# An attention and feed-forward kernel whose program order is planned in advance: new first loads, one weight for all feature products, an added dependency in the plan, new priorities

## The chip, the cores and the metric

The kernel runs on one core of a Trainium2 chip. The metric is the device time of one execution in microseconds (us), as the median of several executions. Beside each changed kernel the kernel before was run on the same chip. PE is the matmul engine, PEld its weight loads, DVE the vector engine, ACT the scalar engine, POOL the general one, and SP issues most transfers.

## The reference, cut to what matters

```python
def _attn_ref(q, k, v, w_phi):               # 8 batches, 8 heads, 576 rows, head_dim 64
    def phi(x):
        proj = einsum('bhsd,df->bhsf', x, w_phi)            # 128 features
        proj = proj - max(abs(proj), axis=-1, keepdims=True)
        return concatenate([exp(proj), exp(-proj)], axis=-1)
    q_p, k_p = phi(q), phi(k)
    kv  = einsum('bhsf,bhsd->bhfd', k_p, v);   z = sum(k_p, axis=2)
    num = einsum('bhsf,bhfd->bhsd', q_p, kv)
    den = einsum('bhsf,bhf->bhs', q_p, z) + 1e-6
    return num / den

def _moe_ref(x, g_ln, w_ch1, w_ch2):         # x: 8 x 576 x 512, all heads side by side
    xn = (x - mean(x)) / sqrt(var(x) + 1e-6) * g_ln
    return x + maximum(xn @ w_ch1, 0) @ w_ch2               # 512 -> 2048 -> 512
```

Inputs and output are fp32; the kernel multiplies in bf16.

## The kernel before

The work is cut into 32 *units* of two heads, eight to each pair of batches. When a pair's eight units are done, its layer norm and its feed-forward block can start. So the units of the second, third and fourth pair run beside the feed-forward products of the pair before. In each unit, k and q are transposed (units 0 to 7 on PE, the later ones by a transposing DMA), multiplied by w_phi into PSUM, and read there. For k, three instructions read the same PSUM tile of 128 x 1024 values: DVE takes the row maxima of the absolute values, and ACT takes exp(+) and exp(-). The exps leave the maximum out; it is put in later as a factor on v, so the first exp does not need it as data.

The order of all this is not written by hand. A small list scheduler in Python (class `Order`) plays the whole kernel through with planned durations, and at each moment gives a free engine the ready operation of the lowest rank. The rank is the latest start that the plan allows plus an offset from a table. When it is done, the operations are emitted in the planned order, and each engine runs its own list in that order on the chip:

```python
class Order:
    def add(self, engine, us, rank, emit, r=(), w=(), acquire=None, release=None, lag=0.2, due=None):
        ...                          # dependencies: on the last writer of every key read or written
    def run(self):
        ...
        for op in done:              # in the order in which the plan started them
            op.emit()
```

These are the operations of a k tile. `us` is the planned duration, `r` and `w` what is read and written. As declared, `exps(0)` and the maxima both only read `ps_key`, so in the plan they may run at the same time:

```python
        add("PE", mm(4, 256), rk(nm, n), products, r=[("qkT", n % QB, i), ("T", n % QB)],
            w=[ps_key] + [("EB", t, n % 2) for t in range(2) if i], acquire=("A", 1))
        add("DVE", 1.14, rk(nm + ".max", n), maxima, r=[ps_key], w=[("m", i, n % 3)],
            release=None if i else ("A", 1))
        ...
        add("ACT", 0.92, rk("k.exp", n), lambda: exps(0), r=[ps_key],
            w=[("EB", 0, n % 2)])
        add("ACT", 0.92, rk("k.exp", n), lambda: exps(1),
            r=[ps_key, ("m", i, n % 3), ("EB", 0, n % 2)],
            w=[("EB", 1, n % 2)], release=("A", 1))
```

And this is the start: w_phi on the POOL queue, three weights made of it, and the first k transpose behind the "mixed" transpose, which needs the tails of q and k (the last 64 rows of each head):

```python
    nc.gpsimd.dma_start(out=wphi_f[0:D, :], in_=w_phi)
    nc.gpsimd.dma_start(out=wphi_f[D : 2 * D, :], in_=w_phi)
    ...
    for nm, s0, s1 in (("wbk", 1.0, 1.0), ("wbx", 2.0, 1.0), ("wbq", 2.0, 2.0)):
        wb[nm] = t_ = consts.tile([P, 2, F], BF16, name=nm)
        ...
        add("PE", mm(1, 128), rank, mixed, r=data, w=[("qxT_ps", n), ("T", j), "T"], acquire=("B", 1))
        ...
        for which in ((1,), (0,)) if n == 0 else ((1, 0),):      # k first, then q
```

## Time and profile before

| | before |
|---|---|
| median time | 409.37 us (408.7 to 410.06, three executions) |
| profiled span | 407.0 us |
| PE busy | 368.2 us, 90 % |
| first k product | 7.99 us |
| first feed-forward product of pair 1, of pair 2 | 49.5 us, 162.4 us |

The page of the profile of the kernel before opens with the span and the busy time of each engine. Then each digit is the busy share, in tenths, of one of 40 equal slices of the span (here 10.2 us each).

```profile
span 407.0 us, 8895 instructions
PE 368.2 (90%) x3315; PEld 232.3 (57%) x3366; DVE 250.2 (61%) x548; ACT 268.7 (66%) x595; POOL 195.5 (48%) x343
...
PE   3998878599999988799999999998999999999994
...
DVE  4688988497989989776666889747373820000000
ACT  3878978379687777674958777867574644444421
```

A 9 is not necessarily full: it means 90 % or more. The view by windows of the kernel before resolves that. Columns: stretch in us, its length, busy us and count of PE, PEld, DVE, ACT and POOL, granted PE clock, mean busy share of the DMA engines, GB/s.

```profile
0.00:50.00 50.00, 41.40 (x670) 37.30 (x677) 36.85 (x86) 37.23 (x82) 33.46 (x78) 1.00 1.00 250
50.00:80.00 30.00, 20.42 (x209) 13.65 (x210) 21.06 (x48) 21.26 (x48) 18.36 (x40) 0.94 1.16 219
80.00:170.00 90.00, 82.65 (x753) 51.11 (x762) 80.54 (x180) 67.61 (x153) 53.94 (x89) 1.00 0.67 170
170.00:230.00 60.00, 56.53 (x512) 35.81 (x522) 42.52 (x83) 42.80 (x95) 32.49 (x52) 1.00 0.52 128
230.00:290.00 60.00, 57.66 (x488) 34.98 (x494) 43.22 (x93) 46.03 (x107) 31.46 (x52) 1.00 0.38 92
```

PE is short of work up to 80 us.

The start on PE, from the timeline of the kernel before (start, duration, engine, line, operation, tiles; in brackets the idle time before and what ended it):

```profile
6.25 0.27 PE L477 MATMUL qxT_ps<-ident,qx_114 128*128 128x128 bf16 x1 [4.43 <-DMA qx_114<-in_k_dram]
...
6.87 0.40 PE L567 MATMUL px<-wbx,qkT_136 128*128 128x256 bf16 x1
...
7.99 1.06 PE L610 MATMUL pm<-wbk,qkT_136 128*128 128x256 bf16 x4
```

PE's two longest waits, from the list of waits of the kernel before (total us, times, longest):

```profile
PE pm L610 <- DMA qkT_136<-b_1_140: 4.9, 1, 4.9
PE qxT_ps L477 <- DMA qx_114<-in_k_dram: 4.4, 1, 4.4
```

The first is the stall near 75 us: one DMA transpose that takes very long. In the chain of waits of the kernel before it is this piece (start, duration):

```profile
59.15 17.20 DMA qkT_136<-b_1_140
```

### The profile page before, as it was taken

What the parts mean: (1) busy time and instruction counts of PE and PEld (TensorE: products, weight loads), DVE (VectorE), ACT (ScalarE), POOL (GpSimd) and SP (SyncE); (2) the same over time, 40 slices, a digit from 0 to 9 for tenths busy, and PEclk for the clock granted to TensorE, in tenths of its full rate; (3) what the DMA queues carried; (4) which work ended last, traced back from release to release, by engine and by line L of the source; (5) the groups of instructions that cost most, each with busy time, mean ns of one, the idle gap of its engine ahead of it and who ended that gap; (6) DMA issues with size and microseconds to landing.
All of it is one profiled execution on the core that took longest, in us unless ns stands there. A gap on an engine that the chain in (4) does not pass through costs nothing.

```text
span 407.0 us, 8895 instructions
## 1 busy us (share of the span) xinstructions
PE 368.2 (90%) x3315; PEld 232.3 (57%) x3366; DVE 250.2 (61%) x548; ACT 268.7 (66%) x595; POOL 195.5 (48%) x343
## 2 busy tenths in 40 slices
PE   3998878599999988799999999998999999999994
PEld 2988845356565645465565655665656555555541
DVE  4688988497989989776666889747373820000000
ACT  3878978379687777674958777867574644444421
POOL 4658768364776726444563744664535211111032
PEclk9999999899999999999999999999999999999998
DMA  7999999957486485966362328421000340101012
GB/s 197 281 228 278 256 229 225 203 157 191 100 226 212 104 219 125 218 104 198 71 195 57 101 78 182 127 52 30 27 28 27 76 119 31 47 27 52 27 52 78
DMA packets 92347, 53.28 MB, mean 131 GB/s; under 512 B 58992, under 2 KB 87664, under 8 KB 92304
## 3 DMA queue, kind: packets, MB, share of 16 engines
q1 hardware_dynamic: 86672, 48.05, 46.6%
q0 software_dynamic: 4288, 4.26, 6.2%
q8 instruction: 26, 0.43, 0.4%
q10 hardware_dynamic: 1344, 0.40, 0.4%
q14 instruction: 17, 0.14, 0.1%
HBM read 36.77 MB, written 9.44 MB: 114 GB/s over the span
## 4 chain that ended last, share of the span: by engine, by line
PE 44%; issue 15%; DVE 15%; DMA 12%; ACT 8%; POOL 3%; SPq 1%; POOLq 0%; ACTq 0%; DVEq 0%
PE hT_ps L989 17%; PE ch_ps L1020 13%; PE pm L610 4%; DMA qkT_136<-b_1_140 4%; ACT eb_141 L627 4%; DMA qkT_138<-b_0_139 3%; ACT eb_142 L627 3%; DVE numc L787 2%; PE n_bank L717 2%; DVE m_144 L617 2%; DVE m_143 L617 2%; POOL o L1039 2%; DVE numc L793 2%; DVE m_145 L617 2%; DMA qk_110<-in_q_dram 1%
## 5 line engine op out<-in xcount | busy, mean ns | idle before, releaser
L1020 PE MATMUL ch_ps<-w_129,hT 128*128 128x512 bf16 x537 | 145.4, 379 | 1.8 <-DVE xT_134 L890 0.2
L989 PEld LDWEIGHTS <-w_128 128*128 128x128 bf16 x768 | 73.2, 98 | 60.6 <-issue 4.5
L999 ACT ACTIVATE hT<-hT_ps 128x384 bf16<-128x384 f32 x127 | 62.5, 492 | 58.6 <-PE hT_ps L989 58.4
L803 POOL TENSOR_TENSOR x<-numc,rden 128x384 bf16<-128x384 f32 (+3 forms) x88 | 45.8, 539 | 76.8 <-DVE rden L797 76.4
L1020 PEld LDWEIGHTS <-hT 128*128 128x128 bf16 x576 | 53.8, 98 | 43.6 <-issue 0.3
L1039 POOL TENSOR_TENSOR o<-o,x 128x512 f32<-128x512 f32 x23 | 26.7, 1159 | 78.0 <-ACT o L1033 72.4
L989 PE MATMUL hT_ps<-xT_135,w_128 128*128 128x384 bf16 x256 | 52.0, 326 | 0.7 <-ACT hT L999 0.7
L989 PE MATMUL hT_ps<-xT_133,w_128 128*128 128x384 bf16 x256 | 50.1, 329 | 2.1 <-ACT hT L999 1.7
L989 PE MATMUL hT_ps<-xT_134,w_128 128*128 128x384 bf16 x256 | 51.2, 326 | 0.5 <-DVE o L1028 0.3
L997 DVE TENSOR_SCALAR hT<-hT_ps 128x384 bf16<-128x384 f32 x65 | 35.8, 553 | 13.5 <-PE hT_ps L989 12.5
L627 ACT ACTIVATE eb_141<-pm 128x1024 bf16<-128x1024 f32 x32 | 32.7, 1029 | 12.4 <-DVE m_144 L617 4.8
L627 ACT ACTIVATE eb_142<-pm 128x1024 bf16<-128x1024 f32 x32 | 32.8, 1026 | 11.5 <-DVE m_143 L617 3.5
L688 ACT ACTIVATE ea_126<-pt 128x1024 bf16<-128x1024 f32 x32 | 32.2, 1047 | 4.4 <-PE pt L682 2.4
L688 ACT ACTIVATE ea_124<-pt 128x1024 bf16<-128x1024 f32 x32 | 32.0, 1039 | 3.4 <-PE pt L682 3.1
L617 DVE TENSOR_REDUCE m_144<-pm 128x8 f32<-128x1024 f32 x22 | 26.8, 1219 | 11.9 <-ACT eb_142 L627 4.7
L617 DVE TENSOR_REDUCE m_143<-pm 128x8 f32<-128x1024 f32 x22 | 26.7, 1217 | 9.8 <-ACT eb_141 L627 6.8
L617 DVE TENSOR_REDUCE m_145<-pm 128x8 f32<-128x1024 f32 x20 | 24.3, 1218 | 10.4 <-PE pm L610 4.2
L1028 DVE SCALAR_TENSOR_TENSOR o<-ch_ps,rstd_165,x 128x512 f32<-128x512 f32 x2 | 1.5, 750 | 41.4 <-PE ch_ps L1020 41.4
L787 DVE TENSOR_TENSOR numc<-num,em 128x390 f32<-128x390 f32 (+1 forms) x40 | 20.6, 514 | 5.8 <-PE num L763 5.6
L1192 PE MATMUL n_bank<-wz 128*128 128x120 bf16 x313 | 22.4, 218 | 1.1 <-DVE KV L725 1.0
L641 POOL TENSOR_TENSOR vv<-v_109,em 128x512 bf16<-128x512 f32 x12 | 12.6, 1049 | 17.9 <-issue 9.2
L793 DVE TENSOR_TENSOR numc<-numc,num 128x390 f32<-128x390 f32 (+1 forms) x40 | 20.5, 515 | 0.3
(221 smaller groups left out, 656.0 us busy)
## 6 DMA issues: line engine op xcount, KB each, us to landing
out_dram<-o SPq DMA_DIRECT2D x32, 256.0 KB, 2.3
qk_108<-in_k_dram SPq DMA_DIRECT2D x12, 256.0 KB, 3.2
v_109<-in_v_dram SPq DMA_DIRECT2D x12, 256.0 KB, 3.8
qk_108<-in_q_dram SPq DMA_DIRECT2D x11, 256.0 KB, 4.8
qk_110<-in_k_dram SPq DMA_DIRECT2D x10, 256.0 KB, 4.5
qk_110<-in_q_dram SPq DMA_DIRECT2D x10, 256.0 KB, 5.7
v_111<-in_v_dram SPq DMA_DIRECT2D x10, 256.0 KB, 4.7
qk_112<-in_k_dram SPq DMA_DIRECT2D x10, 256.0 KB, 4.8
```

Source lines behind the costliest of these rows:

```text
L617: nc.vector.reduce_max(out=u["m"][:, i, 0:MX], in_=u["pm", i], axis=AX.X, apply_absolute_value=True)
L627: nc.scalar.activation(u["EB"][:, t, 0:MX, :], u["pm", 1], AF.Exp, scale=(1.0, -1.0)[t])
L688: nc.scalar.activation(u["EA"][:, t, 0:1024], u["pt"], AF.Exp, scale=(1.0, -1.0)[t])
L787: nc.vector.tensor_tensor(out=view(st["numc"]), in0=view(st["ps"][1]), in1=bcast(e, 3 if shape else 2, D1), op=ALU.mult,)
L793: nc.vector.tensor_add(out=st["numc"], in0=st["numc"], in1=st["ps"][0])
L803: nc.gpsimd.tensor_tensor(out=dst, in0=st["numc"][ps_, i : i + n, 0:D], in1=bcast(st["rden"][ps_, i : i + n], 2, D), op=ALU.mult,)
L989: nc.tensor.matmul(st["ps"], w1_sb[:, kc, jj * P : (jj + 1) * P], xT_bufs[(pair * NR + r) % XB][:, kc::KC, :], start=(kc == 0), stop=(kc = ...
L997: nc.vector.tensor_relu(h_sb, st["ps"])
L999: nc.scalar.activation(h_sb, st["ps"], AF.Relu)
L1020: nc.tensor.matmul(ch[t], hT[r, jj][:, rt * P : (rt + 1) * P], w2_sb[:, jj, :], start=(jj == 0), stop=(jj == JC - 1),)
L1039: nc.gpsimd.tensor_tensor(out=ch["o", t], in0=ch["o", t], in1=x[:, t, :], op=ALU.add)
L1192: nc.tensor.matmul(warm, wz, wz[:, 0:WN], start=False, stop=False, skip_group_check=True)
```

## The change

Its intent is to start the first exps earlier, and to have a better order of work after that. It has four parts. (a) The start: w_phi moves to the ACT queue, and one block-diagonal weight serves all products (q's factor of two goes into a small exp). k transposes no longer wait for tails, the load order is set, and one of two table loads goes away. (b) In the plan, the first exp of k also waits for the maxima. (c) The plan has a new model of how long a transfer holds its queue. (d) All priorities are new.

```diff
-DUE, BLOCK = 34.0, 26.0
+DUE = 24.7
+BLOCK = 127.5
 OFF = (
-        "load": -75.5, "trans": -3.0, "trans.copy": -34.0, "mixed": -14.9, ...
+        "load": 291.2, "trans": 434.7, "trans.copy": 59.4, "mixed": -235.7, ...
   ... (all three tables, every number)
-            us = [2.0 if callable(us) else us for us in op.us]
+            us = [0.6 if callable(us) else us for us in op.us]
-    nc.gpsimd.dma_start(out=wphi_f[0:D, :], in_=w_phi)
-    nc.gpsimd.dma_start(out=wphi_f[D : 2 * D, :], in_=w_phi)
+    nc.scalar.dma_start(out=wphi_f[0:D, :], in_=w_phi)
+    nc.scalar.dma_start(out=wphi_f[D : 2 * D, :], in_=w_phi)
-    wb = {}
-    for nm, s0, s1 in (("wbk", 1.0, 1.0), ("wbx", 2.0, 1.0), ("wbq", 2.0, 2.0)):
-    ...
+    wbk = consts.tile([P, 2, F], BF16, name="wbk")
+    nc.vector.memset(wbk, 0.0)
+    for i in range(2):
+        rows = slice(i * D, (i + 1) * D)
+        nc.vector.tensor_copy(out=wbk[rows, i, :], in_=wphi_f[rows, :])
-        def held(now, free):
-            return max(us, free.get(kind, 0.0) - now)
-        add(queue, held if tiles else us, rank, emit, r=r, w=(key, *w))
+        def issued(now, free):
+            both = free.get(other, 0.0) > now or backlog[other] > 0
+            wait = max(0.0, free.get(kind, 0.0) - now) + backlog[kind] * (0.046 + 0.094 * both)
+            backlog[kind] += packets
+            return max(us, wait) if tiles else us
+        add(queue, issued, rank, emit, r=r, w=(key, *w))
+        if n:
+            add_mixed()
+            add_main((1, 0))
+        else:
+            add_main((1,))         # k block of the first unit
+            add_mixed()
+            add_main((0,))
-                    wbk if i else wbq, start=True, stop=True,
+                    wbk, start=True, stop=True,
-        add("ACT", 0.92, rk("k.exp", n), lambda: exps(0), r=[ps_key],
+        add("ACT", 0.92, rk("k.exp", n), lambda: exps(0), r=[ps_key, ("m", i, n % 3)],
             w=[("EB", 0, n % 2)])
   ... (first loads reordered; one explicit table load)
```

## The prediction

> **What bounds it now.** The page of the profile gives a span of 407.0 us with PE (matmul) busy 368.2 us (90%), ACT 268.7, DVE 250.2. The 10 us windows split it into three stages. (a) 0 to 80 us: PE is often filler or idle; the warm-up matmuls on `wz` (313 of them) fill gaps until 45 us. (b) 80 to about 165 us: PE is mostly busy, but it runs out of feed-forward work at 150 to 170 us (8.21 and 7.72 us busy of 10), because the second pair's attention is not ready; DVE is busy 10.00 of 10 us in 150 to 160. (c) From 170 us PE is nearly full, and from 320 us it is 9.95 of 10. So the end is set by how early the second pair reaches its first feed-forward product (162.4 us in the timeline). That is paced by DVE and ACT, plus stalls.
>
> The stalls that count: the first transpose starts only at 6.25 us (list of waits: PE waits 4.4 us for the `qx` tail load), although the k block, 3.0 to 3.7 us from issue, should be there by about 4.2 us. The first exps of k stand at 10.35 and 13.06 us. At 71.5 to 76.4 us PE waits 4.9 us for the DMA transpose `qkT_136`; in the chain of waits that DMA is 17.2 us long. Its issue alone took 8.1 us, behind 1 MB of loads and beside the w2 load; DMA share is 1.2 to 1.4 there. DVE and ACT idle too (3.9 and 4.0 us busy of 10).
>
> **What the change does.** w_phi goes from the POOL queue to the ACT queue; k transposes no longer wait for tails; six weight scalings on DVE (0.21 to 0.62 us) become two; one table load (1.28 us) goes away. k transposes can start near 4.2 us and k products near 5.3 us instead of 7.99. q now queues behind two w_phi issues (about 0.5 us each) and the mixed tile lands about 1 us later, but that is not first in line now. The Trainium skill (DMA: Bandwidth & Descriptors, "Issuing engines are not separate DMA queues") says that more queues save issue time, not bandwidth; the trace agrees as far as DMA share is already over 1 from 10 us on, so I count only latency. Estimate: 2.5 to 3 us earlier in stage (a). Waiting for the maxima costs the first exp nothing: DVE reads first in any case.
>
> The new order: before the second pair's first centring, DVE work by mean durations is 142.7 us before and 143.6 us after, so no work is saved; ACT is about 4 us lighter. In the new order single loads and DMA transposes alternate on the SP queue, instead of four loads ahead of two transposes, and w2 is asked for earlier. I expect most of the 4.9 us stall to go (3 to 4 us), and 1 to 4 us at the starved passage of 150 to 170 us: the new PE order has feed-forward work of the second pair there one attention group sooner.
>
> **Sum.** 3 + 3.5 + 3 = 9.5 us, less about 1 us for a new wait somewhere; stage (c) is dense in both, so all that is gained by 170 us is kept. Time 400.5 us; range 392 to 408. Faster by over 2%: 0.57; within 2%: 0.40; slower: 0.03.
>
> **Right or wrong:** first k transpose near 4.2 us and first exp near 7.5 us; no PE wait over 2 us on a DMA transpose between 60 and 90 us; first feed-forward product of the second pair by about 155 us; unchanged tail rate.
>
> **What would break it:** k products waiting for w_phi on the ACT queue; the early w2 load and the transposes colliding elsewhere; the early gain absorbed by DVE before 150 us.

## More of the kernel before

The next two fences were not read closely enough before the prediction. They are the timelines of ACT and of DVE in the kernel before, between 208 and 217 us, in the stage called dense:

```profile
209.38 1.02 ACT L627 ACTIVATE eb_141<-pm 128x1024 bf16<-128x1024 f32 x1
211.70 1.02 ACT L627 ACTIVATE eb_141<-pm 128x1024 bf16<-128x1024 f32 x1 [1.29 <-DVE m_144 L617]
...
213.47 1.02 ACT L627 ACTIVATE eb_142<-pm 128x1024 bf16<-128x1024 f32 x1 [0.36 <-PE pm L610]
...
215.78 1.02 ACT L627 ACTIVATE eb_142<-pm 128x1024 bf16<-128x1024 f32 x1 [0.62 <-DVE m_145 L617]
```

```profile
210.44 1.22 DVE L617 TENSOR_REDUCE m_144<-pm 128x8 f32<-128x1024 f32 x1 [1.87 <-ACT eb_141 L627]
...
214.52 1.22 DVE L617 TENSOR_REDUCE m_145<-pm 128x8 f32<-128x1024 f32 x1 [1.36 <-ACT eb_142 L627]
```

Read them together. The first exp runs from 209.38 to 210.40. DVE has waited 1.87 us for it, and takes the maxima from 210.44 to 211.66. Only then, after 1.29 us of idle time, does ACT run the second exp, at 211.70. Three instructions that only read one PSUM tile run strictly one after the other, with DVE in the middle. The plan had the first exp and the maxima side by side.

## The result and the profile after

| | before | after |
|---|---|---|
| median of four executions | 409.42 us (408.7 to 410.06) | 390.84 us (389.74 to 391.21) |
| ratio of the fast runs | | 0.9542 (0.9516 to 0.9568) |
| profiled span | 407.0 us | 388.8 us |
| first k transpose, first k product | 6.31, 7.99 us | 3.53, 5.58 us |
| first exp of k | 10.35 us | 8.88 us |
| first feed-forward product of pair 1, pair 2 | 49.5, 162.4 us | 49.1, 156.1 us |

A ratio, here and below, is the mean time of one kernel's fast runs over that of the other's of the same rounds, so it is not quite the ratio of the medians quoted. The gain is 18.6 us, twice what was forecast, and the time lies below the forecast range. The granted clock of the executions is the same within 1 %.

The same lines of the page, for the kernel after (a slice is 9.7 us):

```profile
span 388.8 us, 8917 instructions
PE 364.6 (94%) x3307; PEld 232.5 (60%) x3354; DVE 255.0 (66%) x556; ACT 259.8 (67%) x576; POOL 201.9 (52%) x348
...
PE   3999995999999989999999999999999999999993
...
DVE  3788995899999999997897998696757000000000
ACT  2877885899786857797976887686946444444411
```

PE's busy time has hardly changed. What went is time in which PE had nothing useful to do. The windows of the kernel after show where:

```profile
0.00:50.00 50.00, 41.52 (x638) 36.71 (x643) 37.43 (x85) 35.07 (x79) 33.32 (x79) 1.00 0.98 249
50.00:80.00 30.00, 24.73 (x246) 16.47 (x247) 23.84 (x54) 22.55 (x56) 21.88 (x45) 0.89 1.02 178
80.00:170.00 90.00, 87.05 (x823) 55.56 (x833) 86.66 (x185) 71.03 (x159) 56.93 (x89) 1.00 0.78 199
170.00:230.00 60.00, 59.52 (x543) 37.66 (x549) 50.74 (x108) 47.87 (x106) 36.63 (x63) 1.00 0.58 130
230.00:290.00 60.00, 59.47 (x587) 38.10 (x596) 44.83 (x99) 42.18 (x100) 37.61 (x62) 1.00 0.28 71
```

Busy time is a blunt measure, since it includes warm-up matmuls that do no work. A sharper one is *lost PE time*: the length of a stretch, less the number of useful matmuls that started in it times the time that one takes when nothing hinders it. The weight loads give the number, one to each matmul. The unhindered times are estimates from dense passages of the traces: 0.65 us for four first feed-forward products, 0.65 us for three second ones, 0.44 us for four products by w_phi, and so on. The useful work comes to 340 to 341 us in every kernel here, so columns can be compared between kernels:

```
lost PE time, us     0-50   50-80  80-170  170-230  230-320    0-320
before               28.9    13.0     9.1      4.4      4.7     60.1
after                29.1     7.9     4.1      0.2      0.3     41.6
gained               -0.2     5.1     5.0      4.2      4.4     18.5
```

The sum of 18.5 us agrees with the 18.2 us between the spans. The start gave nothing, 50 to 80 us and 80 to 170 us gave 5 us each, and the stage that the prediction called dense gave 8.6 us.

The start on PE, from the timeline of the kernel after:

```profile
3.53 0.61 PE L471 MATMUL qkT_ps<-ident,qk_100 128*128 128x128 bf16 x4 [1.99 <-DMA qk_100<-in_k_dram]
5.58 1.03 PE L624 MATMUL pm<-wbk,qkT_128 128*128 128x256 bf16 x4 [1.45 <-DVE qkT_128 L486]
8.39 0.29 PE L479 MATMUL qxT_ps<-ident,qx_106 128*128 128x128 bf16 x1 [1.77 <-DMA vx_107<-in_v_dram]
...
9.03 0.40 PE L581 MATMUL px<-wbk,qkT_128 128*128 128x256 bf16 x1
```

The k products are 2.4 us earlier, but the products of the mixed tile, which hold the tails, are 2.2 us later (9.03 against 6.87 us). The line at 8.39 us names a load of v for its wait; the weight load just before it, whose data this is, waited 2.2 us for q's tails (`qx_106<-in_q_dram`), issued on the ACT queue behind w_phi at 2.64 us. The first unit needs both, and the first product of phi(k) with v starts at 16.0 us, against 15.9 before.

The waits of PE in the kernel after, and the piece of its chain of waits that answers to the stall shown of before:

```profile
PE pm L624 <- DMA qkT_130<-b_0_131: 3.7, 1, 3.7
PE qkT_ps L471 <- DMA qk_100<-in_k_dram: 2.0, 1, 2.0
PE qxT_ps L479 <- DMA vx_107<-in_v_dram: 1.8, 1, 1.8
```

```profile
52.16 15.38 DMA qkT_130<-b_0_131
```

The long DMA transpose is still there. It takes 15.38 us instead of 17.20, and PE waits 3.7 us for it instead of 4.9.

The readers of the k tiles in the same stretch of the kernel after, from the timelines of DVE and then of ACT:

```profile
213.21 1.21 DVE L631 TENSOR_REDUCE m_135<-pm 128x8 f32<-128x1024 f32 x1
```

```profile
214.52 1.94 ACT L643 ACTIVATE eb_133<-pm 128x1024 bf16<-128x1024 f32 x2 [0.43 <-DVE m_135 L631]
```

The maxima come first, and the two exps run as one block ("x2") of 1.94 us. DVE waits for no exp anywhere in this kernel: its list of waits has no such line. Call a unit's exps *split* when its maxima stand between them. In the trace before, 20 of the 32 units are split. In 16 of these ACT was idle just before the second exp, 9.6 us in all; in the other four it had other work there. In the trace after, no unit is split. In the chain of waits of the kernel before, the six readers shown above lie on the chain with 6.6 us between 209.39 and 216.81 us; in the kernel after, the chain between 205 and 220 us is made of PE's matmuls alone. PE's own list of waits between 170 and 320 us agrees. Before, its largest entry is this one, and waits for exps of k come to 3.4 us in all; after, the list is empty.

```profile
PE pm L610 <- ACT eb_141 L627: 2.6, 4, 0.9
```

### The profile page after: what moved, and what is told of

Read it like the earlier page. It is cut to its first block, busy times and chain, and to the rows that moved or that the text cites. A ratio compares the mean times of both kernels' runs of the same rounds, so it can differ in the third digit from the quotient of the medians.

```text
span 388.8 us, 8917 instructions
## 1 busy us (share of the span) xinstructions
PE 364.6 (94%) x3307; PEld 232.5 (60%) x3354; DVE 255.0 (66%) x556; ACT 259.8 (67%) x576; POOL 201.9 (52%) x348
## 4 chain that ended last, share of the span: by engine, by line
PE 57%; issue 21%; DVE 11%; DMA 6%; POOL 3%; ACT 1%; POOLq 0%; SPq 0%; DVEq 0%
PE hT_ps L1006 20%; PE ch_ps L1037 16%; PE pm L624 6%; DMA qkT_130<-b_0_131 4%; PE n_bank L734 3%; POOL o L1056 3%; PE num L780 3%; PE n_bank L1215 2%; PE pt L699 2%; DVE m_137 L631 1%; DVE m_135 L631 1%; DMA qx_106<-in_k_dram 1%; DVE w_120 L451 1%; DVE st_147 L933 1%; PE n_bank L729 1%
## 5 line engine op out<-in xcount | busy, mean ns | idle before, releaser
L1016 ACT ACTIVATE hT<-hT_ps 128x384 bf16<-128x384 f32 x113 | 55.6, 493 | 59.4 <-PE hT_ps L1006 58.9
L1037 PEld LDWEIGHTS <-hT 128*128 128x128 bf16 x576 | 53.3, 98 | 43.8
L1056 POOL TENSOR_TENSOR o<-o,x 128x512 f32<-128x512 f32 x26 | 30.1, 1157 | 85.9 <-ACT o L1050 80.5
L1014 DVE TENSOR_SCALAR hT<-hT_ps 128x384 bf16<-128x384 f32 x79 | 42.9, 549 | 9.8 <-PE hT_ps L1006 9.2
L643 ACT ACTIVATE eb_134<-pm 128x1024 bf16<-128x1024 f32 x32 | 32.8, 1036 | 3.5 <-DVE m_137 L631 1.5
L643 ACT ACTIVATE eb_133<-pm 128x1024 bf16<-128x1024 f32 x32 | 31.7, 1025 | 4.9 <-DVE m_137 L631 3.8
L705 ACT ACTIVATE ea_118<-pt 128x1024 bf16<-128x1024 f32 x32 | 31.9, 1032 | 4.0 <-PE pt L699 2.4
L705 ACT ACTIVATE ea_116<-pt 128x1024 bf16<-128x1024 f32 x32 | 31.5, 1028 | 4.2 <-PE num L786 1.5
L1215 PEld LDWEIGHTS <-wz 128*128 128x128 bf16 x301 | 18.6, 101 | 3.1 <-issue 2.1
```

Source lines behind the costliest of these rows:

```text
L643: nc.scalar.activation(u["EB"][:, t, 0:MX, :], u["pm", 1], AF.Exp, scale=(1.0, -1.0)[t])
L705: nc.scalar.activation(u["EA"][:, t, 0:1024], u["pt"], AF.Exp, scale=(1.0, -1.0)[t])
L1014: nc.vector.tensor_relu(h_sb, st["ps"])
L1016: nc.scalar.activation(h_sb, st["ps"], AF.Relu)
L1037: nc.tensor.matmul(ch[t], hT[r, jj][:, rt * P : (rt + 1) * P], w2_sb[:, jj, :], start=(jj == 0), stop=(jj == JC - 1),)
L1056: nc.gpsimd.tensor_tensor(out=ch["o", t], in0=ch["o", t], in1=x[:, t, :], op=ALU.add)
```

## The experiments

The result raises three questions. Why did the late stage gain? Why did the start give nothing? What of the stall near 64 us? The theory for the first is that part (b) matters because it makes the plan true: the program runs the readers of one PSUM tile in the order in which they were emitted, so a plan that thinks them parallel emits orders that the chip then pays for. Its rivals are that "maxima first" is better in itself, whatever the plan knows; that the better transfers (part c) did it; and that it is just a luckier set of priorities (part d). The texts shorten these theories to letters in places; what each comes to is told below.

All kernels gave correct results except the one that is said to be wrong on purpose. The lost PE time of all of them but a_w2_late, whose trace is not used (experiment 6), in the same columns:

```
lost PE time, us     0-50   50-80  80-170  170-230  230-320
before               28.9    13.0     9.1      4.4      4.7
b_dep                32.3    21.3     8.2      0.6      0.9
b_dep_late           28.9    13.4     4.9      0.8      1.3
b_nudge_late         29.5    13.3     8.2      3.1      4.8
b_flip               28.9    13.2    14.6      5.5      6.7
after                29.1     7.9     4.1      0.2      0.3
a_no_dep             29.4     6.2    18.3      5.6      5.6
a_no_dep_late        29.0    12.0     9.0      3.5      6.3
a_flip               33.7    11.8    24.9     15.2     18.6
a_old_dma            28.3    13.9    10.9      2.1      0.3
a_old_tab            31.3     8.9    13.7      6.3      1.8
a_nudge              28.3    10.5    14.5      2.2      0.5
a_nudge2             29.0    10.8    11.8      1.3      0.9
a_wphi_pool          29.1     8.9     3.9      0.2      1.2
a_wphi_late          32.3     9.2     3.7      0.3      0.3
a_wphi_one           28.1     6.5     3.7      0.4      0.5
a_tails_first        28.6     8.1     3.7      0.3      0.3
a_w2_quarter         28.6     3.2     3.7      0.7      0.2
a_w2_early           31.3     3.2     3.9      0.7      0.3
```

### 1. The dependency taken out, and put in: a_no_dep and b_dep

```diff
 a_no_dep (in after)
-        add("ACT", 0.92, rk("k.exp", n), lambda: exps(0), r=[ps_key, ("m", i, n % 3)],
+        add("ACT", 0.92, rk("k.exp", n), lambda: exps(0), r=[ps_key],
 b_dep (in before)
-        add("ACT", 0.92, rk("k.exp", n), lambda: exps(0), r=[ps_key],
+        add("ACT", 0.92, rk("k.exp", n), lambda: exps(0), r=[ps_key, ("m", i, n % 3)],
```

> The changed kernel, but the planner may again put the first exp of k beside or ahead of the maxima of the same PSUM tile (one dependency taken out of the plan, everything replanned). Theory R (the plan ignored that the two readers of one PSUM tile cannot overlap; a truthful plan is what made the third stage dense): 396 to 402 us, and lost PE time from 170 us on comes back to 4 us or more. Rival T (the new priorities alone did it): within 1% of the changed kernel, 388 to 394 us. Rival D (priorities fit one plan only, any replanning loses): about as much lost as with a meaningless nudge, which is run later.

Measured: 414.06 us, ratio to the kernel before 1.0089 (1.0023 to 1.0155). Without this line the whole gain is gone, and more than the theory had expected (396 to 402 us). But the loss is spread: 14 us in 80 to 170 us, and 5 us in each of the last two stretches.

> The kernel before with that one dependency added to its plan, nothing else. Theory R: 399 to 404 us, the third stage (170 us to the end) loses less than 4 us of PE time where it lost about 9. Rival T: no gain, 407 us or more. Rival D: slower than before, since its priorities were chosen for the other plan.

Measured: 410.95 us, ratio 0.9988 (0.9923 to 1.0053). With the line, the kernel before is no faster, where the theory had 399 to 404 us. The table shows that two effects cancel: the last two stretches lose 0.6 and 0.9 us instead of 4.4 and 4.7, but the first 80 us lose 11.7 us more. The list of waits of b_dep shows a new one:

```profile
PE pm L610 <- DMA qkT<-b: 10.1, 1, 10.1
```

In the replanned order one DMA transpose of the second pair holds PE for 10.1 us, and the first feed-forward product comes at 76.3 us instead of 49.5. One edited line changes the whole plan, for good and ill. A single edit cannot be judged by its total alone.

### 2. The order of the readers turned, with the plan held fixed: a_flip and b_flip

Here the plan is made as it stands, and afterwards only the emission order is re-sorted. Each engine's chain, all data dependencies and all buffer hand-overs are kept. The one edge between the maxima and the first exp of a unit is turned round wherever that closes no circle.

```diff
 a_flip: after the plan is made, per unit
-    maxima -> exps(0)
+    exps(0) -> maxima        (31 of 32 units)
 b_flip: the reverse, in before
-    exps(0) -> maxima
+    maxima -> exps(0)        (the 20 units that had it so; 12 already had maxima first)
```

> The changed kernel with every engine's own order of instructions exactly as it is; only for 31 of 32 units the first exp of k is made to read its PSUM tile before the maxima read it, so DVE waits for ACT there instead of ACT for DVE. It isolates the order of the two readers from any replanning. If the order of readers by itself costs (theory R1): slower by 4 to 10 us, with long waits of DVE maxima for ACT exps. If only the truthfulness of the plan counts (R2): also slower, since the plan assumes maxima first; the two are parted by the mirrored run. If readers do not matter (T): within 1 us.

Measured: 463.39 us, ratio 1.13 (1.1221 to 1.138), 72.6 us more than after. The effect is far above the 4 to 10 us that had been expected. The list of DVE's waits in a_flip has what the kernel after lacks:

```profile
DVE m L689 <- ACT eb L701: 80.5, 30, 5.2
```

Thirty times DVE, which the plan let go first, waits for an exp that stands late in ACT's list, 80.5 us in all. 31 units are split in this trace.

> The kernel before with every engine's own order exactly as it is; for the 20 units of 32 in which the first exp read the PSUM tile before the maxima, the maxima now read first. R1 (maxima first is better in itself): 2 to 6 us faster than before. R2 (the plan must know of it; the tile is held for exp + max + exp either way): within 2 us of before. T: within 1 us.

Measured: 417.82 us, ratio 1.0189 (1.0133 to 1.0245), so 8 us slower, where "maxima first is better in itself" would have it faster. The expectation that the order alone would do it falls. The list of ACT's waits in b_flip:

```profile
ACT eb L685 <- DVE m L675: 45.3, 27, 4.0
```

ACT now waits 45.3 us for maxima, in 27 waits; in the kernel before such waits came to 19.3 us, in 22. The theory that the plan must know had expected to stay within 2 us of the kernel before, so its number failed too. What both runs show is that either order is costly when the plan was made for the other. This speaks for the theory that the plan must know the constraint.

### 3. The dependency from the second pair on only, with a control: b_dep_late, a_no_dep_late, b_nudge_late

To keep the first pair's plan near what it was, the line is changed only for units of the later pairs. Since any edit replans everything after it, the control changes a number of no meaning in the same units: the planned duration of the maxima, 1.20 instead of 1.14 us (measured: 1.22).

```diff
 b_dep_late (in before)
+            r=[ps_key, ("m", i, n % 3)] if n >= 8 else [ps_key],
 a_no_dep_late (in after)
+            r=[ps_key] if n >= 8 else [ps_key, ("m", i, n % 3)],
 b_nudge_late (in before)
+        add("DVE", 1.20 if n >= 8 else 1.14, rk(nm + ".max", n), maxima, ...
```

> The kernel before with the one dependency (first exp of k after its maxima) in its plan, but only for units 8 to 31, so that the plan of the first pair stays as it was. Adding it for all units left the time alone: it took about 14 us of lost PE time away after 110 us, but moved the start of the feed-forward work from 49.5 to 76.3 us. Theory R: the first feed-forward product stays near 50 us, lost PE time from 170 us on is under 3 us as in that run, and the time is 395 to 401 us, most of the gain of the whole change from one line. Rival T (new priorities, new model of transfers are what count): 405 us or more.

Measured: 399.39 us, ratio 0.9751 (0.9689 to 0.9812). One line, for the later units, gives about 10 us. The first 80 us are as before (lost 42.3 against 41.9 us); 80 to 170 us gains 4.2, 170 to 230 us 3.6 and 230 to 320 us 3.4 us. The split units go from 20 to 4. The readers of one tile in this kernel, from its timelines of DVE and of ACT:

```profile
209.01 1.23 DVE L617 TENSOR_REDUCE m<-pm 128x8 f32<-128x1024 f32 x1 [0.66 <-PE pm L610]
```

```profile
210.98 1.96 ACT L627 ACTIVATE eb<-pm 128x1024 bf16<-128x1024 f32 x2
```

> Control for the run in which the dependency alone was added for units 8 to 31: the kernel before, replanned with the maxima of those units at 1.20 us instead of 1.14 in the plan, without the dependency. If the 10 us of that run came from the dependency: this one is 409 us or slower and still loses 4 us or more of PE time from 230 to 320 us. If any replanning of the later units could have given them: 403 us or less.

Measured: 407.54 us, ratio 0.9957 (0.9911 to 1.0003). It had been expected at 409 us or slower, so replanning alone may have given some 2 us. The control keeps 20 split units and the loss in the late stretches. It is one control; how far other meaningless edits of the kernel before would scatter was not measured. The windows of b_dep_late, and then of b_nudge_late, in the columns of above:

```profile
170.00:230.00 60.00, 59.98 (x543) 37.58 (x541) 43.96 (x85) 41.83 (x98) 36.19 (x55) 1.00 0.51 134
230.00:290.00 60.00, 59.35 (x545) 36.60 (x542) 49.27 (x106) 42.51 (x99) 30.96 (x51) 1.00 0.37 89
```

```profile
170.00:230.00 60.00, 57.69 (x515) 36.31 (x521) 46.46 (x88) 45.11 (x104) 33.84 (x56) 1.00 0.57 142
230.00:290.00 60.00, 57.09 (x528) 35.63 (x535) 45.85 (x95) 44.73 (x100) 32.52 (x51) 1.00 0.39 91
```

With the dependency PE is busy 119.3 of 120 us, with the control 114.8.

> The mirror of it: the changed kernel with the dependency taken out of the plan for units 8 to 31 alone. Theory R: the first 60 us are as in the changed kernel, lost PE time after 110 us grows by 8 us or more, 399 to 412 us. Rival T: within 1% of the changed kernel.

Measured: 408.04 us, ratio 0.9952 (0.989 to 1.0014), 17 us above after. 16 units are split again. Of its loss, the part from 230 us on (6.3 us lost against 0.3) is larger than in any run whose plan has the dependency and whose order follows its plan; the part before may be mere replanning, as experiment 5 shows.

What follows: over all the planned kernels, the stretch from 230 to 320 us separates without an exception. With the dependency in the plan it loses 0.2 to 1.8 us, whatever the transfers' model, the priorities or the start are; without it (before, b_nudge_late, a_no_dep, a_no_dep_late), 4.7 to 6.3 us. The two kernels whose order was turned against their plan lose 6.7 and 18.6 us. From 170 to 230 us the two groups are not separate: with the dependency 0.2 to 6.3 us are lost, without it 3.1 to 5.6. So the gain after 230 us is shown to come from the dependency in the plan. The dependency does two things at once: it keeps the readers apart, and it puts the maxima first. b_flip shows that maxima first is not enough when the plan does not know of it. A plan that keeps them apart with an exp first was not tried, so that any such plan would serve is not shown.

### 4. The start: a_wphi_pool, a_wphi_late, a_wphi_one, a_tails_first

```diff
 a_wphi_pool: w_phi back on the POOL queue
-    nc.scalar.dma_start(out=wphi_f[0:D, :], in_=w_phi)      (and the second half)
+    nc.gpsimd.dma_start(out=wphi_f[0:D, :], in_=w_phi)
 a_wphi_late: the same, and issued after POOL's first memsets
 a_wphi_one: one load that reads w_phi twice
+    nc.scalar.dma_start(out=wphi_f,
+        in_=bass.AP(tensor=w_phi.tensor, offset=w_phi.offset, ap=[[0, 2], [F, D], [1, F]]))
 a_tails_first: a_wphi_one, and q's tails issued ahead of q's block
```

> The changed kernel with its two w_phi loads back on the POOL queue, everything else and the order of work on PE, DVE and SP as it is. The q loads then stand first on the ACT queue. If the w_phi queue matters as the change intends: slower by 1 us or more. My reading of the trace is the other way: the first mixed tile waited 1.8 us on PE for the q tails behind the w_phi loads; here it should start about 1.5 us earlier (near 6.8 us instead of 8.4), and the time is between 0 and 2 us better, 0 if the first 50 us absorb such shifts.

Measured: 389.62 us, ratio 0.951 (0.9461 to 0.9558); after has 0.9542. The queue of w_phi does not show in the total. It does show in the first products: those of k come at 7.16 us instead of 5.58, and the mixed transpose at 7.99 us instead of 8.39 (6.8 had been expected). The unchanged total agrees with the Trainium skill (DMA: Bandwidth & Descriptors, "Issuing engines are not separate DMA queues"), by which another issuing engine saves only issue time.

> The changed kernel with w_phi asked for late on purpose, from POOL after its memsets, so that the first products of k start about 3 us later (near 8.5 us instead of 5.6); the order of work on PE and SP is unchanged. If a later start is passed on to the end: 2.5 to 3 us slower. If the first stage absorbs it, since its pace is set by other work up to the first feed-forward product at 49 us: less than 1 us slower, and the first feed-forward product within 1 us of 49.1 us.

Measured: 394.54 us, ratio 0.9631 (0.9578 to 0.9683). The first k product comes at 10.6 us instead of 5.6, the first feed-forward product at 53.3 instead of 49.1, and the last feed-forward product ends 4.3 us later. So the rest of the kernel does pass a delay of the start on. That the change gained nothing at the start because its head start of 2.4 us for k was matched by 2.2 us lost for the tails is argued from the timelines; no run kept the one without the other.

> The changed kernel with one w_phi load that writes both halves from a repeated read, so that the q loads go out 0.6 us earlier on the ACT queue and the second half of w_phi lands 0.5 to 1 us earlier; order of work unchanged on PE, DVE, POOL and SP. A later start was passed on to the end almost in full (w_phi 5 us later: 4 us slower). If an earlier one is passed on too: 0.5 to 1.5 us faster than the changed kernel, the first mixed product at about 8.2 us instead of 9.03. If something else paces the first 50 us: no difference.

> The changed kernel with one w_phi load, and the q tails issued ahead of the q block on the ACT queue, all orders of work else unchanged. The tails then land about 0.6 us earlier, but the transpose that needs them stands behind the k products, which wait for w_phi until 6.6 us, so at most 0.4 us earlier for the first mixed product (8.57 us before). Expected within 1 us of the kernel with one w_phi load alone (388.6 us).

Measured: 388.62 us, ratio 0.9487 (0.9467 to 0.9507), and 390.22 us, ratio 0.9532 (0.9491 to 0.9573). The first mixed product came at 8.57 and at 8.32 us, against 9.03 us after. One issue less on the ACT queue seemed to give 0.5 %, but the kernel that also has the tails earlier does not keep it. The interval of a_wphi_one lies just below that of after (0.9516 to 0.9568, from other rounds), that of a_tails_first covers both. Whether half a per cent is to be had here is not settled.

### 5. The transfers' model and the priorities: a_old_dma, a_old_tab, a_nudge, a_nudge2

```diff
 a_old_dma (in after): held() and 2.0 as in before, no backlog
 a_old_tab (in after): DUE, BLOCK and the three OFF tables of before
 a_nudge (in after), a number of no meaning
-        add("DVE", 1.14, rk(nm + ".max", n), maxima, ...
+        add("DVE", 1.20, rk(nm + ".max", n), maxima, ...
 a_nudge2 (in after), another
-        add("DVE", us, V_dve, total, ...
+        add("DVE", us + 0.01, V_dve, total, ...
```

> The changed kernel with the former model of transfers in its plan (a transpose holds its queue until earlier transfers end, no account of those waiting; 2.0 us as the length of a transfer in the ranks). If the new model is what saved about 5 us of PE time between 50 and 80 us: lost PE time there goes from 8 back to 12 us or more, 395 to 400 us in all. If the plan hardly feels it: within 1% of the changed kernel. Third stage (from 170 us) stays dense in both cases, since the dependency on the maxima is in the plan.

> The changed kernel with the former priorities (the tables of offsets, the due times), all else new. Theory R: the stage from 170 us on is still nearly dense (under 3 us lost), since that comes from the dependency and not from the priorities; the first 100 us may be bad, as when the dependency alone was added to the kernel before for all units (feed-forward work began at 76 us). Expected 400 to 415 us. Rival T: the third stage loses 8 us or more again.

Measured: 407.43 us, ratio 0.9954 (0.9924 to 0.9984), and 410.62 us, ratio 1.0021 (0.9996 to 1.0045). Each undo alone costs nearly the whole gain or all of it. With that of experiment 1 there are thus three parts each of which seems worth 16 us or more, out of 18.6. They cannot all be. a_old_dma had been expected at 395 to 400 us. With the old tables the stretch from 170 us on loses 8.1 us, where the theory had less than 3 and the rival of luckier priorities 8 or more, so on this number the rival was right. But some 4.5 us of it are lost from 170 to 176 us, since the second pair's feed-forward now begins at 175.9 us; from 230 us on 1.8 us are lost.

> Control for every replanned run: the changed kernel with one planning duration moved a little towards what the trace measures (maxima 1.20 us instead of 1.14; the trace has 1.22), which takes away and adds nothing but makes the planner lay out everything anew. Rival D (the priorities fit one plan only, any replanning loses the gain): 400 us or more. If the single undos lost by what they undid: within 1% of the changed kernel, and in any case from 230 to 320 us under 2 us of lost PE time, since the readers' order is in the plan.

> A second control of the same kind: 0.01 us more on the planning duration of the sum of the two numerator halves. Rival D: 400 us or more. Otherwise within 1% of the changed kernel. Under 2 us lost on PE from 230 to 320 us either way.

Measured: 405.78 us, ratio 0.9894 (0.9842 to 0.9947), and 403.53 us, ratio 0.9819 (0.9759 to 0.988). A planned duration that is 0.06 us longer (and nearer to the truth) costs 15 us; one that is 0.01 us longer costs 13. Most of it falls in 50 to 170 us. So both edits that only replan fall to a level of 403.5 to 405.8 us: the priorities of the change seem to fit its one plan. Measured from there, a_old_dma is 2 to 4 us worse, which may be nothing, a_old_tab 5 to 7, and a_no_dep 8 to 10.5. In 50 to 80 us a_old_dma loses 13.9 us, as expected of the old model (12 or more), but the two nudges lose 10.5 and 10.8 us there already. What the nudges do not spoil is the stretch from 230 us on: 0.5 and 0.9 us lost.

### 6. The stall near 64 us: a_w2_quarter, a_w2_early, a_w2_late

In the timeline of the kernel after, the issue of the last w2 loads (512 KB each, from POOL) and that of the long DMA transpose (from SP) stand side by side:

```profile
51.05 2.30 POOL L435 DMA_DIRECT2D w_121<-in_moe_w_ch_dram  x3
52.16 2.38 SPq L560 DMA_TRANSPOSE qkT_130<-b_0_131  x1
```

```diff
 a_w2_quarter: only a quarter of w2 is loaded, the rest is set to zero (wrong result on purpose)
-                out=w2_sb[:, j0 : j0 + JC // NW, :],
+                out=w2_sb[:, j0 : j0 + 1, :],
 a_w2_early, a_w2_late (on a_wphi_one): the four w2 issues moved in POOL's order
+W2_AT = (34.0, 37.0, 40.0, 43.0)        # early; late: (58.0, 60.0, 62.0, 64.0); planned: 47 to 50
```

> Wrong results on purpose: the changed kernel, but each of the four loads of w2 fetches a quarter of its rows, the rest is set to zero at the start; every engine's order of work stays. It asks whether the DMA transpose of the second pair's first head (15.4 us from issue to landing in the changed kernel, 17.2 us for one of its neighbours in the kernel before) is late because w2 streams beside it. If so: it lands within 8 us, PE no longer waits 3.7 us for it near 64 us, and the time falls by 2.5 to 5 us. If it is late because of the loads ahead of it on its own queue: no change beyond 1 us.

Measured: 385.56 us, ratio 0.9413 (0.9391 to 0.9434). The wait for the transpose is gone; the longest of PE's waits in a_w2_quarter are these, both in the first 8 us:

```profile
PE pm L626 <- DVE qkT L488: 3.2, 1, 3.2
PE qkT_ps L473 <- DMA qk<-in_k_dram: 2.0, 1, 2.0
```

50 to 80 us loses 3.2 us instead of 7.9. In the kernel after, the stall is shown to come from w2 streaming beside the transpose, and is worth about 5 us; the kernel before was not tested so. The stall costs PE more than the 3.7 us of its wait. From 66 to 72 us, just after it, the granted PE clock is 0.50 in the kernel after, and four first feed-forward products take 1.48 us at 69.82 us, against 0.81 us at 62.01 us. In a_w2_quarter the clock is 1.00 throughout 50 to 80 us.

> A correct kernel that should beat both: one w_phi load, and the four w2 loads moved ahead in POOL's own order (to where the plan stands at 34, 37, 40 and 43 us, instead of 47 to 50), all other engines' orders unchanged. With a quarter of w2 the transposes came in time and 5 us were gained. If the w2 transfers end before the transposes start and delay nothing else: 382 to 386 us, PE waits under 1 us for a transpose near 64 us. If they only collide with the loads of the first pair instead: 388 us or more and new PE waits before 60 us.

Measured: 388.78 us, ratio 0.9479 (0.9422 to 0.9536). The stall is gone too, but 0 to 50 us loses 31.3 instead of 28.1 us (a_wphi_one), and the total is the same. Among PE's waits in a_w2_early is this new one, for scaled values of v that POOL makes:

```profile
PE n_bank L742 <- POOL vv L679: 2.6, 1, 2.6
```

> The same with the w2 loads moved back (plan times 58 to 64 us), behind the first transposes. The transposes come in time, but the second feed-forward products, which stood at 73.4 us, need w2 at once: expected 386 to 392 us, the wait moved rather than removed, the first such product at 78 us or later.

Measured: ratio 0.9603 (0.9528 to 0.9677) from the fast runs, 393.6 and 394.42 us. Two more executions counted as slow, 400.15 us and one of 987.26 us, which was the profiled one; its trace shows PE slowed everywhere and is not used, and its cause was not looked for. It had been expected at 386 to 392 us. Earlier is no better, and later seems worse, on two fast executions. In a_w2_early, moving the loads moved the wait instead of removing it; for a_w2_late no usable trace shows where the time went. No version here with a right result clearly beats the kernel after.

## Why the prediction was wrong, point by point

- **"stage (c) is dense in both, so all that is gained by 170 us is kept"** is the step that failed most. The stage lost 9.1 us before and 0.5 us after, nearly half of the gain. The 10 us windows that the forecast had read add up to 56.5 and 57.7 us of 60; it took that for full. The error behind it is **"Waiting for the maxima costs the first exp nothing: DVE reads first in any case."** In 20 of 32 units the exp read first, and the maxima then stood between the two exps. What the added wait is worth in the plan, the runs show: for the later pairs alone it gave 10 us (b_dep_late), where a meaningless edit gave 2 (b_nudge_late). For all units, without the new priorities, it gave nothing in total (b_dep).
- **"Estimate: 2.5 to 3 us earlier in stage (a)"** measured 0. The k transposes and products were 2.8 and 2.4 us earlier, as the mechanism had it. But q "is not first in line now" was false: q's loads stood behind two w_phi issues, the mixed transpose waited 2.2 us for q's tails, and the mixed products came 2.2 us later. The first exp came at 8.88 us, not 7.5: its maxima were done at 7.87 us, but ACT's copy of the mixed transpose, at 8.71 us, stood before it. The forecast's remark on the DMA share holds from 10 to 40 us (1.05 to 1.19), not from 40 to 50 us (0.93).
- **"I expect most of the 4.9 us stall to go (3 to 4 us)"**: the wait itself went from 4.9 to 3.7 us only, so the test of no wait over 2 us failed. The stretch from 50 to 80 us gained 5.1 us all the same, because PE had more work before the stall: from 50 to 64 us it was busy 12.6 us, against 9.7 us before. That the sizes are near each other is chance.
- **"1 to 4 us at the starved passage"**: 80 to 170 us gained 5.0, of which the named passage of 150 to 170 us gave 3.8 (4.8 us lost before, 1.0 after). So the size was right, and the second pair's first feed-forward product came at 156.1 us, forecast "by about 155". The mechanism is not shown: in the same passage b_dep_late gains 3.6 us and b_nudge_late 2.5 us, and in b_dep_late that product comes at 163.1 us, later than before.
- **"the early gain absorbed by DVE before 150 us"**, named as a danger, did not happen: a_wphi_late passed its delay on to the end. The tail rate was unchanged, as forecast: PE is busy 9.95 of every 10 us from 320 to 380 us in both kernels.

Still open is how the 5 us of 50 to 80 us, and what of 80 to 170 us is not due to the dependency, divide between the transfers' model and the priorities: every undo replans, and replanning alone costs 13 to 15 us. The 987 us execution of a_w2_late is open as well.

## What to carry to other kernels

If a scheduler plans the order, tell it what cannot run together in the program, as here two readers of one PSUM tile on different engines: look in the timelines for a reduction that stands between two activations of one tile. An engine that is 95 % busy over a long stage is not full; five per cent of 150 us is 7.5 us, more than any single wait of PE listed here before the change. Before you read the undo of one part of a planned kernel, run a meaningless edit as a control, and compare stretches of time rather than totals.

## What the Trainium skill lacked or had wrong

- PSUM — Partial Sum Buffer, "PSUM bank collisions raise a hardware error": it states that two readers of one bank get a dependency, but not its cost. Here exp, maxima and exp of one tile took 1.02, 1.22 and 1.02 us one after the other, ACT was idle for up to 1.29 us in between, and with the order turned against its plan DVE waited 80.5 us in all (a_flip).
- DMA: Bandwidth & Descriptors, "Issuing engines are not separate DMA queues": it says that transfers interleave, but gives no time for what a small one suffers beside a large one. DMA transposes whose median is 3.2 to 5.5 us from issue to landing took 15.4 and 17.2 us beside the 512 KB loads of w2, and the wait vanished when three quarters of w2 were not loaded (a_w2_quarter).
- No page has it: the order of a list-planned kernel is so sensitive that a change of 0.01 us in a planned duration moved the time by 13 us (a_nudge2), so a single undo measures mostly the replanning.
